# Retention by feature: keys in both layouts, queries as the moving operand, heads and gates as column tiles of the array

## The chip, the cores and the metric

The kernel runs on one core of a Trainium2 chip. The metric is the time of one execution on the device in microseconds. Effects of a few microseconds are compared through medians.

In the views PE is TensorE, PEld its weight loads, DVE VectorE, ACT ScalarE, POOL GpSimd. In a matmul the operand `lhsT` is loaded as weights and stays (stationary), while `rhs` streams past (moving). A record is one line of the trace; a float32 matmul of the source leaves two. With the shape of the array I mean rows*columns of the weights, as 128*64 in a view.

## The reference

A retention layer is followed by a mixture of experts with one expert per token. The change concerns the first part and the gate logits.

```python
# q, k, v: (B=8, H=8, S=576, 64)
gamma = 1.0 - 2.0 ** (-5.0 - np.arange(H))
rel = pos[:, None] - pos[None, :]
Dmat = np.where(rel >= 0, gamma[:, None, None] ** rel, 0.0)
ret = (q @ k.T / 8) * Dmat
x = (ret @ v)                      # then (B, S, 512)
logits = x @ w_gate                # 8 experts
local_gate = sigmoid(x @ w_local)  # 1 more column
# ... each token through relu(x @ w1[e]) @ w2[e], times its softmax share
```

## The kernel before

The 4608 tokens go in 36 chunks of 128; nine chunks are a pair of sequences. The decay gamma^(t-s) is split into a factor on the queries' side and one on the values. So a chunk needs masked scores times values inside the chunk, queries times a running state for what came before, and an update of that state. Everything is float32. The parts that the change touches:

```python
def scores(i):
    ld = raw.tile([P, 3, D], F32)              # q by feature; k, v by token
    nc.sync.dma_start(out=ld, in_=qkv[i])
    for c in range(4):                         # keys by feature, on TensorE
        nc.tensor.transpose(kps[:, c, :], kn[:, c * P:(c + 1) * P], ident)
    nc.scalar.copy(kT, kps)
    # vs = v * key decay (GpSimd)
    for c in range(4):
        for u in range(2):                     # two heads in two row halves
            nc.tensor.matmul(sps[u][:, c, :], lhsT=kT[r, c, :], rhs=qT[r, c, :], ...)
    # sT = sps * mask (VectorE)

def outputs(i):
    for h in range(8):                         # scores stationary, values moving
        nc.tensor.matmul(ops[:, h, :], lhsT=sT[:, h % 2, h // 2, :],
                         rhs=vs[:, h * DH:(h + 1) * DH], ...)
    for c in range(4):                         # queries stationary, state moving
        nc.tensor.matmul(ops[...], lhsT=qT[:, c, 0:n], rhs=state[:, c, :], ...)
    for c in range(4):                         # two heads against two: half is thrown away
        nc.tensor.matmul(kv[:, c, :], lhsT=kn[r, c * P:(c + 1) * P],
                         rhs=vs[r, c * P:(c + 1) * P], ...)
    # state = diagonal blocks of kv (ScalarE); x = ops * query decay; x to DRAM

def logits(i):
    for c in range(4):
        nc.tensor.transpose(xps[:, c, :], x[:, c * P:(c + 1) * P], ident)
    nc.scalar.copy(xT, xps)
    for c in range(4):
        nc.tensor.matmul(lps[:, i, :], lhsT=xT[:, c, :], rhs=wg[:, c, :], ...)
# cut: the routing (which expert each token takes), then 25 blocks of 256 slots through experts
```

## Time and profile before

| | before |
|---|---|
| median of 4 runs, us | 1038.82 (1037.56 to 1039.0) |
| retention, to the last gate matmul | 250.3 us |
| routing and experts | the rest, 787 us |

Two groups of retention in the costliest-groups view, and the load of a chunk in the list of DMA issues. In a group, the shapes after the names are weights and moving operand (partitions x elements). Then come the count of records, busy time in us, mean ns of one, idle time before them and what ended it.

```profile
L139 PE MATMUL ops<-vs,sT 128*128 128x64 f32 x576 | 82.3, 277 | 0.0
L112 PE MATMUL kps<-ident,ld 128*128 128x128 f32 x144 | 22.6, 281 | 6.2 <-DMA ld<-in_qkv_dram 6.2
...
ld<-in_qkv_dram SPq DMA_DIRECT2D x36, 768.0 KB, 4.5
```

The first is the target: 576 records of intra-chunk outputs, each loading 128 columns of weights to stream only 64. The second is the key transposes. Neither waits for anything after the first loads. The third tells that a chunk's load lands in 4.5 us, while a chunk takes 6.6.

### The profile page before, as it was taken

How to read it: one execution, taken by the hardware profiler on the slowest of the kernel's cores; microseconds unless marked ns; L12 is line 12 of the kernel's file. 1: busy time of each engine (PE TensorE's matmuls, PEld its weight loads, DVE VectorE, ACT ScalarE, POOL GpSimd, SP SyncE). 2: the span in 40 equal slices, each digit the busy share in tenths (PEclk: the TensorE clock that was granted, in tenths of full speed). 3: DMA queues.
4: the chain of work that ended last, by engine and by line, in shares of the span. 5: the costliest groups of instructions: out<-in, count | busy, mean ns of one | idle time of the engine just before them, and what ended most of it. 6: DMA issues, size and time to landing. Idle time of an engine off the chain costs nothing. (4 is left out here: it accounts for less than half of the span.)

```text
span 1037.5 us, 12062 instructions
## 1 busy us (share of the span) xinstructions
PE 974.9 (94%) x4918; PEld 719.0 (69%) x4918; DVE 166.8 (16%) x282; ACT 123.8 (12%) x238; POOL 140.7 (14%) x158
## 2 busy tenths in 40 slices
PE   7999999996479999999999999999999999999995
PEld 6999999995466666666666666666666666666662
DVE  2333332324711111010111111010111110010100
ACT  2222222221000000000000000000000000000000
POOL 2111111110021111011111110011111110110000
PEclk9999999998589999999999999999999999999998
DMA  5444444430735544555455544555455544555300
GB/s 201 154 158 157 151 163 162 163 133 32 273 122 203 201 156 148 185 197 177 153 179 187 193 156 153 181 193 188 138 187 203 164 158 160 195 183 167 127 2 0
DMA packets 47509, 166.03 MB, mean 160 GB/s; under 512 B 7006, under 2 KB 7134, under 8 KB 47456
## 3 DMA queue, kind: packets, MB, share of 16 engines
q1 hardware_dynamic: 39168, 142.62, 40.5%
q0 software_dynamic: 8000, 22.56, 6.3%
q8 instruction: 39, 0.64, 0.2%
q14 instruction: 14, 0.11, 0.0%
q10 hardware_dynamic: 288, 0.09, 0.0%
HBM read 146.37 MB, written 22.54 MB: 163 GB/s over the span
## 5 line engine op out<-in xcount | busy, mean ns | idle before, releaser
L395 PE MATMUL hps<-xTs,w1s 128*128 128x256 f32 x1600 | 353.2, 382 | 14.1 <-DVE xTs L389 14.1
L402 PE MATMUL yps<-w2s,hT 128*128 128x512 f32 x800 | 347.4, 592 | 0.0
L395 PEld LDWEIGHTS hps<-xTs,w1s 128*128 128x128 f32 x1600 | 303.0, 191 | 60.2 <-DVE xTs L389 19.8
L402 PEld LDWEIGHTS yps<-w2s,hT 128*128 128x128 f32 x800 | 152.0, 190 | 180.7 <-issue 179.4
L405 DVE TENSOR_SCALAR y<-yps,pslot 128x512 f32<-128x512 f32 x50 | 37.5, 751 | 665.4 <-PE yps L402 665.4
L397 ACT ACTIVATE hT<-hps 128x512 f32<-128x512 f32 x100 | 59.7, 597 | 700.2 <-PE hps L395 700.2
L406 POOL DMA_INDIRECT out_dram<-y,sidx x50 | 50.7, 1014 | 512.0 <-DVE y L405 505.3
L139 PE MATMUL ops<-vs,sT 128*128 128x64 f32 x576 | 82.3, 277 | 0.0
L139 PEld LDWEIGHTS ops<-vs,sT 128*128 128x128 f32 x576 | 72.4, 191 | 4.9 <-issue 0.6
L127 DVE TENSOR_TENSOR sT<-sps,mask 128x512 f32<-128x512 f32 x72 | 46.4, 686 | 159.9 <-PE sps L123 159.9
L383 POOL DMA_INDIRECT xg<-xd,gidx x50 | 48.7, 975 | 164.0 <-PE xgps L388 121.2
L116 POOL TENSOR_TENSOR vs<-ld,dec 128x512 f32<-128x512 f32 x36 | 37.5, 1042 | 190.0 <-PE kv L155 173.2
L123 PE MATMUL sps<-ld,kT 64*128 64x128 f32 x576 | 43.2, 288 | 0.2 <-DVE sT L127 0.2
L161 ACT COPY state<-kv 64x256 f32<-64x256 f32 x64 | 23.4, 366 | 160.2 <-PE kv L155 159.4
L176 PE MATMUL lps<-wg,xT 128*128 128x9 f32 x288 | 38.0, 259 | 1.5 <-ACT xT L174 1.1
L176 PEld LDWEIGHTS lps<-wg,xT 128*128 128x128 f32 x288 | 34.9, 191 | 5.2 <-ACT xT L174 4.7
L123 PEld LDWEIGHTS sps<-ld,kT 64*128 64x128 f32 x576 | 36.3, 190 | 2.9 <-DVE sT L127 0.4
L388 PEld LDWEIGHTS xgps<-ident,xg 128*128 128x128 f32 x200 | 24.2, 146 | 20.1 <-issue 19.5
L155 PE MATMUL kv<-vs,ld 128*128 128x128 f32 (+1 forms) x256 | 35.5, 281 | 0.5 <-ACT state L161 0.5
L146 PE MATMUL ops<-state,ld 128*128 128x128 f32 (+1 forms) x256 | 35.4, 281 | 0.0
L388 PE MATMUL xgps<-ident,xg 128*128 128x128 f32 x200 | 27.7, 282 | 6.6 <-DMA xg<-xd,gidx 6.6
L389 DVE COPY xTs<-xgps 128x512 f32<-128x512 f32 x50 | 32.2, 682 | 7.1 <-PE xgps L388 7.1
(112 smaller groups left out, 271.2 us busy)
## 6 DMA issues: line engine op xcount, KB each, us to landing
w1s<-in_w_dram SPq DMA_DIRECT2D x100, 512.0 KB, 5.5
w2s<-in_w_dram SPq DMA_DIRECT2D x100, 512.0 KB, 8.1
ld<-in_qkv_dram SPq DMA_DIRECT2D x36, 768.0 KB, 4.5
xd<-x SPq DMA_DIRECT2D x36, 256.0 KB, 2.2
xg<-xd,gidx POOLq DMA_INDIRECT x50, 7.3
out_dram<-y,sidx POOLq DMA_INDIRECT x50, 7.5
dec<-in_decay_dram ACTq DMA_DIRECT2D x1, 72.0 KB, 4.6
wg<-in_wgl_dram ACTq DMA_DIRECT2D x1, 18.0 KB, 6.2
```

Of the source, the lines that this page charges most:

```text
L116: nc.gpsimd.tensor_tensor(vs.rearrange("p (h d) -> p h d", h=H), vn.rearrange("p (h d) -> p h d", h=H), dec[:, 1, m, :].unsqueeze(2).to_br ...
L123: nc.tensor.matmul(sps[u][:, c, :], lhsT=kT[r, c, :], rhs=qT[r, c, :], start=True, stop=True, skip_group_check=True)
L127: nc.vector.tensor_tensor(sT[:, u], sps[u], (mask2 if m == MID else mask).unsqueeze(1).to_broadcast([P, HP, P]), op=Alu.mult)
L139: nc.tensor.matmul(ops[:, h, :], lhsT=sT[:, h % 2, h // 2, :], rhs=vs[:, h * DH:(h + 1) * DH], start=(h == 0), stop=(m == 0), skip_group_c ...
L176: nc.tensor.matmul(lps[:, i, :], lhsT=xT[:, c, :], rhs=wg[:, c, :], start=(c == 0), stop=(c == DK - 1), skip_group_check=True)
L383: nc.gpsimd.indirect_dma_start(out=xg, out_offset=None, in_=xd, in_offset=bass.IndirectOffsetOnAxis(ap=gidx[:, s:s + 1], axis=0))
L388: nc.tensor.transpose(xps[:, c, :], xg[:, c * P:(c + 1) * P], ident)
L395: nc.tensor.matmul(hps[:, v, :], lhsT=w1s[:, m + v, c, :], rhs=xT[:, c, :], start=(c == 0), stop=(c == DK - 1), skip_group_check=True)
L397: nc.scalar.activation(hT[:, m:m + 2, :], hps, Act.Relu)
L402: nc.tensor.matmul(yps, lhsT=hT[:, m, u * P:(u + 1) * P], rhs=w2s[:, m, :], start=(m == 0), stop=(m == FK - 1))
L405: nc.vector.tensor_scalar(y, yps, pslot[:, s:s + 1], None, Alu.mult)
L406: nc.gpsimd.indirect_dma_start(out=out, out_offset=bass.IndirectOffsetOnAxis(ap=sidx[:, s:s + 1], axis=0), in_=y, in_offset=None, bounds_c ...
```

## The change: its intent and the diff

The products are turned round so that what is small becomes the weights. Values (64 columns) are stationary and scores move. Two heads then fit side by side in the left and right 64 columns of the array. The output comes by feature, as the gates need it, and is transposed to tokens for the store instead. Keys are loaded in both layouts, so no key is transposed on the chip. The gates' four partial products are four 32-column tiles, summed by one more matmul a chunk later.

```diff
-            ld = raw.tile([P, 3, D], F32, name="ld")
+            ld = raw.tile([P, 4, D], F32, name="ld")
-            for c in range(HP):
-                nc.tensor.transpose(kps[:, c, :], kn[:, c * P:(c + 1) * P], ident)
-            nc.scalar.copy(kT, kps)
+            kT = ld[:, 1].rearrange("p (c s) -> p c s", c=HP)
 ...
-            for h in range(H):
-                nc.tensor.matmul(ops[:, h, :], lhsT=sT[:, h % 2, h // 2, :],
-                                 rhs=vs[:, h * DH:(h + 1) * DH], ...)
+            for c in range(HP):
+                for u in range(2):
+                    r = slice(u * DH, (u + 1) * DH)
+                    h = 2 * c + u
+                    nc.tensor.matmul(ops[r, c, :], lhsT=vs[:, h * DH:(h + 1) * DH], rhs=sT[:, u, c, :], ...)
 ...
-                        lhsT=qT[:, c, 0:n], rhs=states[(i + 1) % 2][:, c, :],
+                    nc.tensor.matmul(ops[:, c, 0:n], lhsT=states[(i + 1) % 2][:, c, :], rhs=qT[:, c, 0:n], ...)
 ...
-                    nc.tensor.matmul(kv[:, c, :], lhsT=kn[r, c * P:(c + 1) * P],
-                                     rhs=vs[r, c * P:(c + 1) * P], ...)
+                    for u in range(2):      # r: rows of the output, h: one head, k: tokens
+                        nc.tensor.matmul(kv[r, c, :], lhsT=kn[k, h], rhs=vs[k, h], ...)
 ...
+        def rows(i):
+            for c in range(DK):
+                nc.tensor.transpose(xps[:, c, :], xT[:, c, :], ident)
+            nc.scalar.copy(x, xps.rearrange("p c d -> p (c d)"))
+            nc.sync.dma_start(out=xd[i * P:(i + 1) * P, :], in_=x)
+            for c in range(DK):
+                nc.tensor.matmul(gps[c * GW:(c + 1) * GW, :], lhsT=wg[:, c, :], rhs=xT[:, c, :], ...)
+            nc.scalar.copy(gs, gps)
         def logits(i):
+            nc.tensor.matmul(lps[:, i, :], lhsT=chunks[i]["gs"], rhs=four[:, 0:E + 1], ...)
```

The query decay, now along the free axis, is a table of nine pieces of 256 KB that is loaded at the start.

More of the change, by code (lines that the diff above doesn't have):

```diff
@@ L38 @@
 NOWHERE = 2 * NTOK
+GW = 32
 @with_exitstack
@@ L45 @@
     qkv: bass.AP,
-    decay: bass.AP,
+    dk: bass.AP,
+    dq: bass.AP,
     wgl: bass.AP,
@@ L75 @@
         work = pool(part, "work", 3)
-        ps_t = pool(part, "ps_t", 2, PSUM)
         ps_s = pool(part, "ps_s", 3, PSUM)
         ps_o = pool(part, "ps_o", 1, PSUM)
+        ps_x = pool(part, "ps_x", 1, PSUM)
+        ps_g = pool(part, "ps_g", 1, PSUM)
         ps_kv = pool(part, "ps_kv", 1, PSUM)
         ps_l = pool(part, "ps_l", 1, PSUM)
-        dec = once.tile([P, 2, PER, H], F32, name="dec")
-        nc.scalar.dma_start(out=dec.rearrange("p t m h -> p (t m h)"), in_=decay)
-        wg = once.tile([P, DK, E + 1], F32, name="wg")
+        deck = once.tile([P, PER, H], F32, name="deck")
+        nc.scalar.dma_start(out=deck.rearrange("p m h -> p (m h)"), in_=dk)
+        decq = once.tile([P, PER, HP, P], F32, name="decq")
+        for m in range(PER):
+            nc.scalar.dma_start(out=decq[:, m].rearrange("p c t -> p (c t)"), in_=dq[:, m])
+        wg = once.tile([P, DK, GW], F32, name="wg")
         nc.scalar.dma_start(out=wg.rearrange("p k e -> p (k e)"), in_=wgl)
+        four = once.tile([P, GW], F32, name="four")
+        nc.gpsimd.memset(four, 0.0)
+        for k in range(DK):
+            nc.vector.tensor_copy(four[k * GW:(k + 1) * GW], ident[k * GW:(k + 1) * GW, k * GW:(k + 1) * GW])
         mask = once.tile([P, P], F32, name="mask")
@@ L105, in scores @@
             g = chunks[i]
-            ld = raw.tile([P, 3, D], F32, name="ld")
+            ld = raw.tile([P, 4, D], F32, name="ld")
             nc.sync.dma_start(out=ld.rearrange("p t x -> p (t x)"), in_=qkv[i])
             qT = ld[:, 0].rearrange("p (c s) -> p c s", c=HP)
-            kn, vn = ld[:, 1], ld[:, 2]
-            kps = ps_t.tile([P, HP, P], F32, name="kps", tag="t")
-            for c in range(HP):
-                nc.tensor.transpose(kps[:, c, :], kn[:, c * P:(c + 1) * P], ident)
-            kT = work.tile([P, HP, P], F32, name="kT")
-            nc.scalar.copy(kT, kps)
+            kT = ld[:, 1].rearrange("p (c s) -> p c s", c=HP)
+            kn, vn = ld[:, 2], ld[:, 3]
             vs = work.tile([P, D], F32, name="vs")
@@ L117, in scores @@
                 vs.rearrange("p (h d) -> p h d", h=H), vn.rearrange("p (h d) -> p h d", h=H),
-                dec[:, 1, m, :].unsqueeze(2).to_broadcast([P, H, DH]), op=Alu.mult)
+                deck[:, m, :].unsqueeze(2).to_broadcast([P, H, DH]), op=Alu.mult)
             sps = [ps_s.tile([P, HP, P], F32, name=f"sps{u}", tag="s") for u in range(2)]
@@ L136, in outputs @@
             qT, kn, vs, sT = g["qT"], g["kn"], g["vs"], g["sT"]
-            ops = ps_o.tile([P, H, DH], F32, name="ops")
-            for h in range(H):
-                nc.tensor.matmul(ops[:, h, :], lhsT=sT[:, h % 2, h // 2, :],
-                                 rhs=vs[:, h * DH:(h + 1) * DH],
-                                 start=(h == 0), stop=(m == 0), skip_group_check=True)
+            ops = ps_o.tile([P, HP, P], F32, name="ops")
+            for c in range(HP):
+                for u in range(2):
+                    r = slice(u * DH, (u + 1) * DH)
+                    h = 2 * c + u
+                    nc.tensor.matmul(ops[r, c, :], lhsT=vs[:, h * DH:(h + 1) * DH], rhs=sT[:, u, c, :],
+                                     start=(c == 0), stop=(m == 0), skip_group_check=True)
             if m > 0:
@@ L145, in outputs @@
                 for c in range(HP):
-                    nc.tensor.matmul(
-                        ops[0:n, 2 * c:2 * c + 2, :].rearrange("p h d -> p (h d)"),
-                        lhsT=qT[:, c, 0:n], rhs=states[(i + 1) % 2][:, c, :],
-                        start=False, stop=True, skip_group_check=True)
+                    nc.tensor.matmul(ops[:, c, 0:n], lhsT=states[(i + 1) % 2][:, c, :], rhs=qT[:, c, 0:n],
+                                     start=False, stop=True, skip_group_check=True)
@@ L150, in outputs @@
             if m != PER - 1:
-                r = slice(HALF, P) if m == MID else slice(0, P)
+                k = slice(HALF, P) if m == MID else slice(0, P)
                 if m in (0, MID):
-                    kv = ps_kv.tile([P, HP, P], F32, name="kv")
+                    kv = ps_kv.tile([P, HP, DH], F32, name="kv")
                 for c in range(HP):
-                    nc.tensor.matmul(kv[:, c, :], lhsT=kn[r, c * P:(c + 1) * P],
-                                     rhs=vs[r, c * P:(c + 1) * P],
-                                     start=(m in (0, MID) and c == 0), stop=True,
-                                     skip_group_check=True)
+                    for u in range(2):
+                        r = slice(u * DH, (u + 1) * DH)
+                        h = slice((2 * c + u) * DH, (2 * c + u + 1) * DH)
+                        nc.tensor.matmul(kv[r, c, :], lhsT=kn[k, h], rhs=vs[k, h],
+                                         start=(m in (0, MID) and c == 0), stop=True,
+                                         skip_group_check=True)
@@ L159, in outputs @@
                 for u in range(2):
                     r = slice(u * DH, (u + 1) * DH)
-                    nc.scalar.copy(states[i % 2][r, :, r], kv[r, :, r])
-            g["x"] = x = work.tile([P, D], F32, name="x")
-            nc.vector.tensor_tensor(
-                x.rearrange("p (h d) -> p h d", h=H), ops,
-                dec[:, 0, m, :].unsqueeze(2).to_broadcast([P, H, DH]), op=Alu.mult)
-            nc.sync.dma_start(out=xd[i * P:(i + 1) * P, :], in_=x)
-        def logits(i):
-            x = chunks[i]["x"]
-            xps = ps_t.tile([P, DK, P], F32, name="xps", tag="t")
-            for c in range(DK):
-                nc.tensor.transpose(xps[:, c, :], x[:, c * P:(c + 1) * P], ident)
-            xT = work.tile([P, DK, P], F32, name="xT")
-            nc.scalar.copy(xT, xps)
-            for c in range(DK):
-                nc.tensor.matmul(lps[:, i, :], lhsT=xT[:, c, :], rhs=wg[:, c, :],
-                                 start=(c == 0), stop=(c == DK - 1), skip_group_check=True)
+                    nc.scalar.copy(states[i % 2][r, :, r], kv[r, :, :])
@@ new lines, in outputs @@
+            g["xT"] = xT = work.tile([P, HP, P], F32, name="xT")
+            nc.vector.tensor_tensor(xT, ops, decq[:, m], op=Alu.mult)
+        def rows(i):
+            xT = chunks[i]["xT"]
+            xps = ps_x.tile([P, DK, P], F32, name="xps")
+            for c in range(DK):
+                nc.tensor.transpose(xps[:, c, :], xT[:, c, :], ident)
+            x = work.tile([P, D], F32, name="x")
+            nc.scalar.copy(x, xps.rearrange("p c d -> p (c d)"))
+            nc.sync.dma_start(out=xd[i * P:(i + 1) * P, :], in_=x)
+            gps = ps_g.tile([P, P], F32, name="gps")
+            for c in range(DK):
+                nc.tensor.matmul(gps[c * GW:(c + 1) * GW, :], lhsT=wg[:, c, :], rhs=xT[:, c, :],
+                                 start=True, stop=True, skip_group_check=True)
+            gs = work.tile([P, P], F32, name="gs")
+            nc.scalar.copy(gs, gps)
+            chunks[i]["gs"] = gs
@@ L179 @@
+        def logits(i):
+            nc.tensor.matmul(lps[:, i, :], lhsT=chunks[i]["gs"], rhs=four[:, 0:E + 1],
+                             start=True, stop=True, skip_group_check=True)
         scores(0)
-        for i in range(NCH + 1):
+        for i in range(NCH + 2):
             if i + 1 < NCH:
@@ L184 @@
                 outputs(i)
-            if i > 0:
-                logits(i - 1)
+            if 0 <= i - 1 < NCH:
+                rows(i - 1)
+            if 0 <= i - 2 < NCH:
+                logits(i - 2)
         nc.vector.tensor_copy(lt, lps)
@@ L422, in _decay @@
 def _decay(np):
-    at = (np.arange(PER)[None, :] * P + np.arange(P)[:, None]) % S
+    at = np.arange(PER * P) % S
     gamma = 1.0 - 2.0 ** (-5.0 - np.arange(H))
-    power = gamma[None, None, :] ** at[:, :, None].astype(np.float64)
-    both = np.stack([power / math.sqrt(DH), 1.0 / power], 1)
-    return both.reshape(P, 2 * PER * H).astype(np.float32)
+    power = gamma[:, None] ** at[None, :].astype(np.float64)
+    dq = (power / math.sqrt(DH)).reshape(HP, 2, 1, PER, P) * np.ones((1, 1, DH, 1, 1))
+    dq = dq.transpose(1, 2, 3, 0, 4).reshape(P, PER, HP * P)
+    dk = (1.0 / power).reshape(H, PER, P).transpose(2, 1, 0).reshape(P, PER * H)
+    return dk.astype(np.float32), dq.astype(np.float32)
 def kernel(**inputs):
@@ L438 @@
     i = {n: _np.asarray(a) for n, a in inputs.items()}
-    gates = _np.concatenate([i["moe_w_gate"], i["moe_w_local"]], 1)
+    gates = _np.concatenate(
+        [i["moe_w_gate"], i["moe_w_local"], _np.zeros((D, GW - E - 1), _np.float32)], 1)
+    dk, dq = _decay(_np)
     arrays = {
         "qkv": _np.concatenate(
-            [_by_feature(i["q"], _np), _by_token(i["k"], _np), _by_token(i["v"], _np)], 2),
-        "decay": _decay(_np),
-        "wgl": gates.reshape(DK, P, E + 1).transpose(1, 0, 2).reshape(P, DK * (E + 1)),
+            [_by_feature(i["q"], _np), _by_feature(i["k"], _np),
+             _by_token(i["k"], _np), _by_token(i["v"], _np)], 2),
+        "dk": dk,
+        "dq": dq,
+        "wgl": gates.reshape(DK, P, GW).transpose(1, 0, 2).reshape(P, DK * GW),
         "w1": i["moe_w1"].reshape(E, DK, P, FK, P).transpose(0, 2, 3, 1, 4).reshape(E, P, FK * D),
```

## The prediction

> **What bounds the kernel now.** I read the page first, its line of busy tenths: it shows three stages. These are the first ten slices (a slice is 1037.5 / 40 = 26 us), a dip, and the experts. The change touches the first stage, retention, alone.
>
> ```profile
> PE   7999999996479999999999999999999999999995
> ...
> PEclk9999999998589999999999999999999999999998
> ```
>
> TensorE is at 9 (90% or more) in both long stages, at full clock. The dip is the routing, on VectorE. The busy time of every engine in a stretch of 26 us in mid-retention says what limits that stage:
>
> ```profile
> 130.00:156.00 26.00, 25.96 (x250) 24.83 (x249) 7.83 (x12) 6.60 (x16) 4.12 (x4) 1.00 0.50 166
> ```
>
> The columns are PE, PEld, DVE, ACT, POOL, then granted clock, DMA share, GB/s. PE is busy for 25.96 of 26 us; the vector engines are below a third, DMA at half. So what a part of the change saves or costs on PE moves the end, and nothing else does, as long as no engine or queue comes near PE. Next, the timeline of PE over one whole chunk of 128 tokens:
>
> ```profile
> 112.28 1.16 PE L123 MATMUL sps<-ld,kT 64*128 64x128 f32 x16
> 113.37 0.66 PE L139 MATMUL ops<-vs,sT 128*128 128x64 f32 x4
> 113.86 1.11 PE L146 MATMUL ops<-state,ld 128*128 128x128 f32 x8
> 114.81 1.06 PE L155 MATMUL kv<-vs,ld 128*128 128x128 f32 x8
> 115.70 0.60 PE L172 MATMUL xps<-ident,x 128*128 128x128 f32 x4
> 116.14 0.60 PE L112 MATMUL kps<-ident,ld 128*128 128x128 f32 x4
> 116.58 0.78 PE L139 MATMUL ops<-vs,sT 128*128 128x64 f32 x6
> 117.38 1.06 PE L176 MATMUL lps<-wg,xT 128*128 128x9 f32 x8
> 118.29 0.86 PE L139 MATMUL ops<-vs,sT 128*128 128x64 f32 x6
> 119.08 1.16 PE L123 MATMUL sps<-ld,kT 64*128 64x128 f32 x16
> ```
>
> The first column is the start; since durations overlap, I take differences of starts. There is no wait in it: one chunk is 119.08 - 112.28 = 6.80 us of 64 records. A matmul of the source is two records in float32 (8 score matmuls, x16), a transpose is one. The records cost what their weights cost, not what they stream: lps with 9 moving columns takes 0.91 / 8 = 0.114 us, kv with 128 takes 0.89 / 8 = 0.111. Over nine chunks (first and last of a pair of sequences do less) stores of x go out at 108.92 and 168.60: 59.68 / 9 = 6.63 us a chunk. The last gate matmul ends at 250.3.
>
> Two exceptions carry my argument. **The scores run in pairs already.** They have K = 64 and alternate between the two halves of the rows: x16 takes 1.09 us, 0.068 each. In the trace their single starts are 7 ns apart within a pair, 112 ns from pair to pair. **One 64-column tile alone gains nothing, and a switch costs.** At the chunk of two sequences the state product has 64 weight columns, all in one half of the array:
>
> ```profile
> 100.08 1.09 PE L146 MATMUL ops<-state,ld 128*64 128x128 f32 x8
> 101.10 1.16 PE L155 MATMUL kv<-vs,ld 64*128 64x128 f32 x8
> 102.18 0.66 PE L172 MATMUL xps<-ident,x 128*128 128x128 f32 x4
> ```
>
> These take 1.02 and 1.08 us, where the full shapes take 0.95 and 0.89. From single starts there, 64-column records come 109 ns apart, set by the 128 moving columns; at each change of array shape one step is some 200 ns rather than 112, and the next 160 to 207. So a change of shape costs 0.14 to 0.19 us, 0.15 as my mean.
>
> **What the Trainium skill says.** (1) "TensorE: Matmul & The Clock Gate", section LDWEIGHTS: a load takes columns / 1.2 ns whatever K is, so 107 ns for 128 and 53 for 64. The trace agrees on the first (0.111 a record, weight-bound). (2) The same page, Part 3, measured speedup: three 32-column tiles with N = 512 gained 2.38x, about as row tiles do. This trace has the row tiles; it has no two column tiles together, so concurrency in float32 is an extrapolation. (3) "TensorEngine Tiling (Array Packing)", Key Properties: changing the tiling mode drains TensorE. The trace agrees, with the 0.14 to 0.19 us above. (4) "DMA: Bandwidth & Descriptors", Queues, rings and completion order: an engine takes turns between queue rows a packet at a time. This matters for the start only; no run before shows two loaded queues there.
>
> **The change part by part**, in PE time of a chunk, at 0.112 us a full record or a pair of tiles.
> - Scores: unchanged, 8 pairs, 0.90.
> - Key transposes removed, as keys come by feature too: before 0.44, after 0. An ACT copy of 0.59 goes with them.
> - Intra-chunk outputs: weights are now values with 64 columns, moving is the score tile of 128, two heads in two column halves. Before 16 records x 0.112 = 1.79; after 8 pairs x 0.112 = 0.90 if the halves overlap.
> - State product: roles swapped, still full, 8 x 0.112 = 0.90; 0.80 on average over nine chunks, as one has none.
> - kv: before 8 full records, 0.89, half of whose product was thrown away. After, 16 records of 64 x 64 in pairs. Weights and stream are both 53 ns, so 8 x 0.056 = 0.45 at best; if issue binds (the scores issue a load or matmul each 28 ns) 32 x 0.028 = 0.90. I take 0.65, so 0.58 on average.
> - Transposes of x stay, 0.44, now from feature to token, and ACT copies x out of PSUM for the store.
> - Gates: before 8 full records, 0.89. After, 8 records in four 32-column tiles: 2 x 0.112 = 0.22 at best, 0.45 if issue binds (I take 0.33), an ACT copy of 128x128, and one matmul to sum the four, 2 x 0.112 = 0.22.
> - Shape changes: before two of weight per chunk, into and out of the scores, part of the 6.63. After, the compiled order of PE is scores, ops, state, kv, xps, gps, lps, never interleaved: 7 changes in a chunk, 5 where state or kv is missing, so 6.6 x 0.15 = 0.98.
>
> Sum: 0.90 + 0.90 + 0.80 + 0.58 + 0.44 + 0.33 + 0.22 + 0.98 = 5.15 us, against 6.63. That is 1.48 us less; over the 34 chunks between the second store and the last, 50 us.
>
> Beside PE, per chunk: DVE keeps three passes of 0.69, 2.07; ACT has 2 x 0.37 + 0.59 + about 0.3 = 1.65; POOL 1.04. All are far below 5.15. Walking through the order with one PSUM buffer each for ops, xps, gps and kv, every reader is done more than 1.5 us before PE wants the buffer again. Gates are summed one chunk later than made, so lps finds its copy ready. I expect no wait of PE on an engine.
>
> DMA: a chunk loads 1.05 MB rather than 0.79 and stores 0.26: 1.31 MB / 5.15 us = 254 GB/s. Before, 166 GB/s were a share of 0.50; linearly 0.77.
>
> Start: at the start of before, loads of 768 KB were first used at 5.34, 7.26 and 9.15 us, so one each 1.9 us (414 GB/s). After, loads of 1 MB take 2.5 us alone, or 5 while 2.36 MB of query decay (nine DMAs) share the engines. The first scores then start at about 7.5 us, the second at 12, the third at 16; but no transpose and copy precede them. The second chunk's x would be ready at about 20 us; before, its store went out at 22.1. So about 2 us more gain, and the tail (about 3 us) is as before. In all 52 us, less 1 for what I overlook: 1039 - 51 = **988 us**. Routing and experts are untouched.
>
> **The rivals.**
> (a) Column tiles don't overlap in float32: matmuls in the two halves follow each other at 0.109. Then ops cost 1.75, gates 0.87, kv 0.90: 5.15 + 0.85 + 0.54 + 0.28 = 6.82 a chunk, 0.2 above before, so about 1043 us: within 2%. For it: the lone 64-column tile above gained nothing. Against: row halves overlap fully here. Chance 0.1.
> (b) Shape changes cost more with column tiles, say 0.30 each, with a weight load of every tile exposed: 1 us more a chunk, 1024 us, within 2%. For it: steps of 207 ns follow the drain of row tiles. Chance 0.07 in full; in part it is the upper end of my range.
> (c) DMA becomes the bound: 1.31 MB at the 330 GB/s that a share of 1.0 would give (166 / 0.50) is 4.0 us, below 5.15. Then nothing is lost; but if PE were as quick as 4.8 it would still not bind. I give it the start, 3 to 5 us. Slower than before would need 36 chunks at 200 GB/s: chance 0.02.
> (d) No issue limit, cheap switches (0.10): 5.15 - 0.2 - 0.1 - 0.33 = 4.5 us a chunk, 965 us. Chance 0.08.
>
> **Range and chances.** The known parts of the sum (scores, ops, state, transposes, lps) are 3.26 us; the doubtful ones (kv, gates, switches) are 1.89, uncertain by about +0.5 and -0.4, so +17 and -14 us. The range is 974 to 1008. Faster by over 2% means below 1018: all of my case, and part of (b). Chances 0.88, 0.09, 0.03.
>
> **What would show it.** Right: retention's last gate matmul ends near 199 us rather than 250; PE still above 95% busy in mid-retention; ops x16 in about 0.9 us plus a switch, starts in pairs; kv x16 between 0.5 and 0.9; DMA share 0.7 to 0.8. Wrong: ops x16 near 1.8 us (rival a); gaps above 0.25 us at each change of shape (b); scores waiting on a load in mid-retention (c); PE waiting on ACT for xps or gps, which I excluded. The expert stage should last as long as before; if it doesn't, my reading that the stages are separate is wrong.

## More of the kernel before

The kernel before was less steady: in one call 6 of its 11 runs took 1045 us and 5 took 1038 to 1040, in another 2 of 7 took 1045, all at granted clocks of 0.977 to 0.981.

## The result and the profile after

The changed kernel took 979.04 us (median of 4 runs, 977.95 to 982.49) against 1038.82. The ratio is 0.9432, 95% interval 0.9414 to 0.9449. A ratio here is the mean time of one kernel's fast runs over that of the other's in the same rounds, so it is not quite the ratio of the two medians. The time lies 9 us below the predicted 988, inside its range.

The busy tenths of TensorE, and every engine's busy time in the same stretch as before (PE, PEld, DVE, ACT, POOL, clock, DMA share, GB/s):

```profile
PE   6999999727999999999999999999999999999995
```

```profile
130.00:156.00 26.00, 26.00 (x370) 21.68 (x370) 10.46 (x16) 8.20 (x22) 5.21 (x5) 1.00 0.80 269
```

The first stage is now nearly eight slices of 24 us (190.8 us), and TensorE is still busy throughout it but for the start. It has 370 records in 26 us instead of 250. DMA is at 0.80, and between 30 and 180 us the trace shows no wait of TensorE's matmuls for a load. One chunk with all its parts, on the timeline of PE (start, duration):

```profile
106.38 1.16 PE L131 MATMUL sps<-ld 64*128 64x128 f32 x16
107.47 1.09 PE L151 MATMUL ops<-sT,vs 128*64 128x128 f32 x16
108.49 1.16 PE L157 MATMUL ops<-ld,state 128*128 128x128 f32 x8
109.58 0.69 PE L167 MATMUL kv<-vs,ld 128*64 128x64 f32 x16
110.20 0.65 PE L180 MATMUL xps<-ident,xT 128*128 128x128 f32 x4
110.78 0.42 PE L186 MATMUL gps<-xT,wg 128*32 128x128 f32 x8
111.14 0.39 PE L193 MATMUL lps<-four,gs 128*128 128x9 f32 x2
111.46 1.16 PE L131 MATMUL sps<-ld 64*128 64x128 f32 x16
```

The chunk takes 111.46 - 106.38 = 5.08 us instead of 6.80. The 16 intra-chunk records take 1.02 us with one change of shape; before they took 2.08 in three pieces. The 16 key-value records take 0.62 us. In the trace's single starts, the intra-chunk records come in pairs 7 ns apart, 109 ns from pair to pair; the key-value ones in pairs every 58 ns; the gates four at a time within 20 ns, the second four starting 133 ns after the first.

The start looks different. From the full timeline:

```profile
5.88 2.08 PE L131 MATMUL sps<-ld 64*128 64x128 f32 x16 [5.88 <-DMA ld<-in_qkv_dram]
...
9.05 2.67 PE L131 MATMUL sps<-ld 64*128 64x128 f32 x16 [1.09 <-DMA ld<-in_qkv_dram]
...
16.85 2.08 PE L131 MATMUL sps<-ld 64*128 64x128 f32 x16 [2.38 <-DMA ld<-in_qkv_dram]
...
20.76 1.88 PE L157 MATMUL ops<-ld,state 128*128 128x128 f32 x8
...
22.68 0.69 DVE L174 TENSOR_TENSOR xT<-ops,decq 128x512 f32<-128x512 f32 x1 [2.46 <-PE ops L157]
```

The bracket is the idle time before the group and what ended it. TensorE waits for the second and third chunk. The group of 16 that takes 1.16 us in mid-stage takes 2.08 here, and the state product 1.88 instead of 1.16: the array runs at half pace. The trace's clock records begin, at full clock, 22.3 us into the span; in the kernel before they begin at 11.1. This one profile is not the whole story, as the part on the start shows.

### The profile page after: what moved, and what is told of

The parts are those of the page before. It is cut to its first block, busy times and chain, and to the rows that moved or that the text cites. A ratio compares the mean times of both kernels' runs of the same rounds, so it can differ in the third digit from the quotient of the medians.

```text
span 977.2 us, 12437 instructions
## 1 busy us (share of the span) xinstructions
PE 913.9 (94%) x5102; PEld 641.8 (66%) x5102; DVE 167.0 (17%) x286; ACT 112.1 (11%) x238; POOL 140.3 (14%) x159
## 5 line engine op out<-in xcount | busy, mean ns | idle before, releaser
L414 PE MATMUL hps<-xTs,w1s 128*128 128x256 f32 x1600 | 353.0, 381 | 14.1 <-DVE xTs L408 14.1
L124 POOL TENSOR_TENSOR vs<-ld,deck 128x512 f32<-128x512 f32 x36 | 37.5, 1042 | 136.2 <-DMA ld<-in_qkv_dram 92.4
L131 PE MATMUL sps<-ld 64*128 64x128 f32 x576 | 45.2, 297 | 9.3 <-DMA ld<-in_qkv_dram 9.3
L131 PEld LDWEIGHTS sps<-ld 64*128 64x128 f32 x576 | 38.0, 199 | 10.7 <-DMA ld<-in_qkv_dram 7.3
L151 PE MATMUL ops<-sT,vs 128*64 128x128 f32 x576 | 41.1, 287 | 0.0
L157 PE MATMUL ops<-ld,state 128*128 128x128 f32 (+1 forms) x256 | 37.6, 291 | 0.0
L157 PEld LDWEIGHTS ops<-ld,state 128*128 128x128 f32 x256 | 31.7, 195 | 5.6 <-issue 5.6
L151 PEld LDWEIGHTS ops<-sT,vs 128*64 128x64 f32 x576 | 32.1, 141 | 4.5 <-issue 0.4
L174 DVE TENSOR_TENSOR xT<-ops,decq 128x512 f32<-128x512 f32 x36 | 24.9, 691 | 31.4 <-PE ops L157 30.4
L367 PE MATMUL slots<-col,row 128*128 128x100 f32 x72 | 11.1, 331 | 13.6 <-DVE col L358 13.6
```

The lines of the kernel that those rows point to most:

```text
L124: nc.gpsimd.tensor_tensor(vs.rearrange("p (h d) -> p h d", h=H), vn.rearrange("p (h d) -> p h d", h=H), deck[:, m, :].unsqueeze(2).to_broa ...
L151: nc.tensor.matmul(ops[r, c, :], lhsT=vs[:, h * DH:(h + 1) * DH], rhs=sT[:, u, c, :], start=(c == 0), stop=(m == 0), skip_group_check=True)
L157: nc.tensor.matmul(ops[:, c, 0:n], lhsT=states[(i + 1) % 2][:, c, :], rhs=qT[:, c, 0:n], start=False, stop=True, skip_group_check=True)
L414: nc.tensor.matmul(hps[:, v, :], lhsT=w1s[:, m + v, c, :], rhs=xT[:, c, :], start=(c == 0), stop=(c == DK - 1), skip_group_check=True)
```

## The experiments

All kernels gave the right result. Differences are from the changed kernel, 979.04 us (978.44 in the rows after_again to late_decay).

| label | what | median us | difference |
|---|---|---|---|
| ops_serial | loop of the output heads turned | 994.04 | +15.0 |
| kv_serial | loop of the key-value heads turned | 986.77 | +7.7 |
| gates_full | gates as before | 981.87 | +2.8 |
| keys_back | keys transposed on chip | 996.75 | +17.7 |
| after_again | unaltered | 978.44 | 0 |
| kv_first | 5 changes of shape for 7 | 971.53 | -6.9 |
| four_switches | 4 changes for 7 | 964.34 | -14.1 |
| late_decay | decay table loaded piece by piece | 972.35 | -6.1 |
| ops_split | output halves kept apart | 1009.23 | +30.2 |
| kv_full | key-value products as before | 984.28 | +5.2 |
| best1 | four_switches and late_decay | 959.87 | -19.2 |
| best2 | best1, first loads in two pieces | 964.75 | -14.3 |

My theory: the gain comes from column halves running at once, from the key transposes left out, and less from the rest; changes of the array's shape take part of it back. The main rivals are that narrow weights alone are the gain, and that the gaps between groups are waits that would be there anyway.

### Do the halves run at once? ops_serial, kv_serial, ops_split

The first try turned the loop, so that neighbours share a half:

```diff
-            for c in range(HP):
-                for u in range(2):
+            for u in range(2):
+                for c in range(HP):
```

> The changed kernel with one loop turned round: the intra-chunk products of the even heads (left 64 columns) all come before those of the odd heads (right 64 columns). Same instructions, same shapes. Theory (the gain comes from two halves of the array running at once, which needs neighbours in different halves): the 16 records of a chunk follow each other at 0.109 us instead of going in pairs, 1.74 us instead of 0.87, so +0.87 us a chunk, 36 chunks: +31 us, about 1010 us. Rival (the gain is from the narrower weights alone, or the array overlaps whatever the order): 979 us, unchanged.

It took 994.04 us, half of the expected loss, between theory and rival. The timeline of PE shows why:

```profile
109.39 1.25 PE L151 MATMUL ops<-sT,vs 128*64 128x128 f32 x13
110.38 0.27 PE L167 MATMUL kv<-vs,ld 128*64 128x64 f32 x1
110.48 0.27 PE L151 MATMUL ops<-sT,vs 128*64 128x128 f32 x1
110.49 0.22 PE L167 MATMUL kv<-vs,ld 128*64 128x64 f32 x1
110.59 0.27 PE L151 MATMUL ops<-sT,vs 128*64 128x128 f32 x1
```

In the program, all 16 output records precede the key-value records. In the trace, key-value records of the left half start between the last output records of the right half. One half overtakes the other, measured against the order of the program. Whether the array does this or the compiled order of instructions is not shown: the compiled order is not on record, and it moves matmuls elsewhere (late_decay below). Among the outputs too, single starts show five left records alone, 109 ns apart, then right ones joining 6 ns behind. So turning the loop did not take the overlap away, only part of it, and this run alone could not decide.

> The same turn of the loop for the key-value state alone (64 weight columns, 64 moving). Theory: the records follow each other at 0.058 us, 16 in 0.93 us instead of 0.46, in 32 of 36 chunks: +15 us, about 994. If a half cannot load its next weights while it streams, up to 0.11 a record and +28 us or so more. Rival (already limited by the issue of instructions): unchanged, 979.

The same turn for the key-value products cost 7.7 us, again half of what I expected, and their single starts overtake in the same way. A chunk with all parts took 115.27 - 109.91 = 5.36 us on its timeline instead of 5.08.

So a third kernel put full-array work between the halves:

```diff
-            for c in range(HP):
-                for u in range(2):      # both halves of the outputs
             # state product first, start=(c == 0)
+            intra(0)                    # left half
+            rows(i - 1)                 # the transposes of the chunk before
+            intra(1)                    # right half
```

> The changed kernel with the two halves of the intra-chunk outputs really apart: the four heads of the left half, then the transposes of the chunk before (full array), then the four heads of the right half; the state product goes ahead of both. Same instructions, same result, 7 changes of shape in a chunk with all parts as before (one or two more at the ends of a pair of sequences, 0.05 us a chunk on average). Full-array work between keeps one half from overtaking the other, as it did when only the loop was turned. Theory: 16 records one after another at 0.109, +0.87 us a chunk, up to 0.2 given back by the key-value products overtaking: 24 to 33 us more, 1002 to 1012 us. Rival (narrow weights are the gain): 979 to 981.

```profile
112.50 1.09 PE L152 MATMUL ops<-sT,vs 128*64 128x128 f32 x8
113.52 0.66 PE L185 MATMUL xps<-ident,xT 128*128 128x128 f32 x4
114.10 1.09 PE L152 MATMUL ops<-sT,vs 128*64 128x128 f32 x8
115.12 0.42 PE L194 MATMUL gps<-xT,wg 128*32 128x128 f32 x8
```

Now 8 records take as long (1.02 us each group) as the 16 did. A full chunk elsewhere in this trace took 110.32 - 104.38 = 5.94 us, 0.86 more than 5.08, for the 0.87 of the theory. The loss is 30.2 us; theory said 24 to 33, the rival 0 to 2. The narrow weights by themselves gain nothing for the outputs: the overlap of the two halves is worth 30 us of the 60.

### What the other parts are worth: keys_back, kv_full, gates_full

keys_back loads three layouts again and transposes keys two chunks ahead, beside the state product:

```diff
+            kn, vn = ld[:, 1], ld[:, 2]
+            for c in range(HP):
+                nc.tensor.transpose(kps[:, c, :], kn[:, c * P:(c + 1) * P], ident)
+            nc.scalar.copy(kT, kps)
```

> The changed kernel with keys loaded by token alone and transposed on TensorE again, two chunks ahead, next to the state product so that no change of array shape is added (only in the 4 to 8 chunks without a state product). Theory (PE-bound; keys by feature save just the four transposes): +0.44 us a chunk, +16 us, less 1 to 3 us for a start with a quarter less to load: 992 to 995. Rival 1 (the larger loads cost what the transposes saved): 979 or less. Rival 2 (the copy of the transposed keys on ScalarE was a wait of its own): over 1000.

It took 996.75 us, 2 above my range. A full chunk took 108.90 - 103.43 = 5.47 us on its timeline, 0.39 more than 5.08. From the second chunk's x to the last chunk's a chunk took 5.245 us on average for 4.856, over 34 chunks 13.2 us. The other 4.8 us of the trace's loss lie before the second x, where I expected a gain:

```profile
12.68 1.28 ACT L125 ACT_TABLE_LOAD   x1 [12.68 <-DMA decq<-in_dq_dram]
13.97 1.07 ACT L125 COPY kT<-kps 128x512 f32<-128x512 f32 x2
...
14.61 5.01 PE L140 MATMUL sps<-ld,kT 64*128 64x128 f32 x32 [3.51 <-ACT kT L125]
```

ScalarE issues the nine loads of the decay table before it copies the first keys. So the first scores started at 14.61 us instead of 5.88, after a wait of 3.51 us for that copy: rival 2 was true at the start, and only there. Part of the 4.8 us is this wait and part the first transposes themselves; the run doesn't tell their shares apart. DMA fell from 0.81 to 0.59 of its time between 52 and 156 us without any use. So the larger load is free there. The transposes are worth 13 us from the second x on, and less than 18 in all.

kv_full goes back to eight full key-value records, half thrown away:

```diff
-                    for u in range(2):
-                        nc.tensor.matmul(kv[r, c, :], lhsT=kn[k, h], rhs=vs[k, h], ...)
+                    nc.tensor.matmul(kv[:, c, :], lhsT=kn[k, c * P:(c + 1) * P], rhs=vs[k, c * P:(c + 1) * P], ...)
```

> The changed kernel with the key-value products as before, 8 full records of which half is thrown away, instead of 16 in two 64-column halves. Theory: 0.89 instead of 0.46 us, but in the 28 chunks that have a state product two changes of shape fall away, 0.30: 28 x 0.13 + 4 x 0.43 = 5 us more, about 984. Rival (changes of shape cost nothing): 32 x 0.43 = 14 us more, 993.

984.28 us, as the theory has it and not the rival. On its timeline a full chunk takes 112.48 - 107.27 = 5.21 us. Half the records cost almost as much as the tiles here, because the tiles need a change of shape on each side.

> The changed kernel with the gates computed as before (the token-feature tile stationary, nine gate columns moving, 8 full records), so no 32-column tiles, no copy of their result, no summing matmul. Theory: 0.89 us of full records takes the place of 0.22 + 0.22 and of two changes of array shape, 0.30: +0.15 us a chunk, +5 us, 984. Rival (changes of shape cost nothing, the four tiles are all gain): +0.45 us a chunk, +16 us, 995.

The gates as before (edit: the eight full records of the old logits read xT, and the tiles, their copy and the summing matmul go) took 981.87 us, +2.8 for the expected +5. On its timeline a chunk takes 114.02 - 108.82 = 5.20 us, 0.12 more for the expected 0.15, which would be 4.3 us over 36 chunks. Most of the remaining 1.5 is in the tail: without the extra step for the sum, the last gate matmul ended 1.39 us after the last x instead of 2.36. The four tiles, which look like a large saving, are worth almost nothing where they stand.

### Do the changes of shape cost time by themselves? kv_first, four_switches

kv_first moves the key-value products up, next to the outputs of the same shape; not one instruction is added or removed:

```diff
-            if m > 0:                   # state product
-                ...
             if m != PER - 1:            # key-value products
                 ...
+            if m > 0:
+                ...
```

four_switches also puts the summing gate matmul before the gate tiles, next to the transposes:

```diff
             rows(i - 1)                 # transposes only
             logits(i - 2)               # the summing matmul
+            gates(i - 1)                # the four tiles
```

> The changed kernel once more, unaltered, so that the small differences of this call are taken on one chip: 977 to 982 us.

The unaltered kernel took 978.44 us (976.08 to 980.68).

> The changed kernel with the key-value products moved from behind the state product to before it, next to the intra-chunk products of the same array shape. Nothing else changes; a chunk that has both then changes the array's shape 5 times instead of 7 (28 of 36 chunks). Theory (each change costs about 0.15 us by itself): 28 x 2 x 0.15 = 8 us less, about 971. Rival (the gaps at the borders of groups are waits for semaphores or the first weights, and come with every group whatever its shape): unchanged, 979.

> As kv_first, and the summing gate matmul of the chunk two back, a full shape, goes before the four-column-tile gates instead of behind them, next to the transposes of the same shape: 4 changes of shape instead of 7. Theory: 36 x 0.15 = 5 us more than kv_first, about 965 us. Rival: unchanged, 979.

They took 971.53 and 964.34 us: 6.9 and 14.1 less. Below is a chunk of four_switches on the timeline of PE, from outputs to the next scores.

```profile
108.47 1.09 PE L151 MATMUL ops<-sT,vs 128*64 128x128 f32 x16
109.39 0.64 PE L161 MATMUL kv<-vs,ld 128*64 128x64 f32 x16
109.95 1.16 PE L168 MATMUL ops<-ld,state 128*128 128x128 f32 x8
110.95 0.60 PE L181 MATMUL xps<-ident,xT 128*128 128x128 f32 x4
111.39 0.29 PE L197 MATMUL lps<-four,gs 128*128 128x9 f32 x2
111.60 0.43 PE L190 MATMUL gps<-xT,wg 128*32 128x128 f32 x8
111.96 1.16 PE L131 MATMUL sps<-ld 64*128 64x128 f32 x16
```

Outputs now take 109.39 - 108.47 = 0.92 us where 1.02 were, transposes 0.44 where 0.58 were: the gap is gone wherever the next group has the same shape, and stays where it has not. The groups and their dependencies are the same, so the rival falls. The chunk is 111.96 - 107.37 = 4.59 us against 5.08: three changes fewer save 0.49, so 0.16 each. In kv_first it is 112.55 - 107.77 = 4.78, 0.30 less for two changes.

### The start: late_decay, and the best versions

```diff
-        for m in range(PER):
-            nc.scalar.dma_start(out=decq[:, m]..., in_=dq[:, m])
             nc.sync.dma_start(out=ld..., in_=qkv[i])
+            if i < PER:
+                nc.sync.dma_start(out=decq[:, i]..., in_=dq[:, i])
```

> The changed kernel with each 256 KB piece of the query decay loaded behind the chunk that needs it, on the same queue, instead of nine at the very start on another queue. Theory (they share the engines with the first three chunks, TensorE waits 1.1 and 2.4 us more for these and then runs some microseconds at half pace): the second and third chunk land at about 8 and 12 us instead of 9 and 17, 4 to 6 us less, about 974. Rival (the first chunks land no sooner, as 1 MB each is what takes the time): 978 to 979.

It took 972.35 us, 6.1 less than after_again, where 4 to 6 were expected.

```profile
8.07 1.11 PE L167 MATMUL kv<-vs,ld 128*64 128x64 f32 x14
9.42 1.98 PE L131 MATMUL sps<-ld 64*128 64x128 f32 x16 [0.24 <-DMA ld<-in_qkv_dram]
...
13.80 1.16 PE L131 MATMUL sps<-ld 64*128 64x128 f32 x16
```

The third chunk's scores start at 13.80 us rather than 16.85 and run at full pace; the clock records begin at 11.2 us. Two things came together here. The table no longer competes with the chunks' loads, and the compiled order moved 14 key-value records ahead of the second scores, which filled the gap. This run does not tell their shares apart. Against the expectation the second chunk landed no sooner (its scores start at 9.42 us, before at 9.05); only the third did.

How long the half pace lasts is not fixed by the kernel alone. after_again, the same kernel, was at full clock from 13.9 to 17.3 us, then at half until 20.7, and its second x was ready at 22.35 us rather than 23.37. The runs with the early decay table (keys_back apart, whose start differs) can be sorted by the idle time of TensorE before the third scores. Where it was 2.3 to 3.1 us (the two of the changed kernel, gates_full, kv_serial, kv_first, four_switches), half pace lasted or came back until 20.7 to 23.3 us. Where it was 1.5 to 1.6 us (ops_serial, ops_split, kv_full), the clock was full from 14.9 to 15.9 us on; kv_full, for one:

```profile
16.82 1.16 PE L131 MATMUL sps<-ld 64*128 64x128 f32 x16 [1.53 <-DMA ld<-in_qkv_dram]
```

So a longer gap and half pace go together in nine profiles. No run changed the gap alone.

> four_switches and late_decay together. Theory (one shortens every chunk, the other the start): 14 + 6 = 20 us less than the changed kernel, 958 to 960. Rival (the shorter chunk makes the loads the bound): 964 as with four_switches alone.

best1 took 959.87 us, as the sum said. It beats the changed kernel by 19 us and the kernel before by 78 (against the lower of two clusters of before; the ratio, 0.9211, is flattered by the upper one). In the stretch from 26 to 156 us its DMA share is 0.92 at 305 GB/s, and beside the first load the waits of its scores for loads sum to 1.4 us. Of these 1.1 lie after 26 us, where the changed kernel has none: a sign, not a proof, that the loads are the next bound.

> best1 with the first two chunks' loads in two pieces each, queries and keys by feature first, so that the first scores start about 1 us sooner: 957 to 959. If the first scores still wait for the whole, as best1.

best2 (first two loads split in two) failed: 964.75 us. The first scores did start sooner, at 5.24 us for 5.93. But the compiled order then spread the second chunk's work so that the clock records begin at full clock only at 17.8 us, not 10.6, and outputs of 16 records took 1.97 us meanwhile. Its second x was ready at 22.49 us for 17.93, which is nearly the whole loss. Why the half pace lasted so long is not shown; a wait of 1.36 us for the second load stood in it, where best1 waited 0.25.

## Why the prediction was right, point by point

**What bounds.** Right. Retention is bound by TensorE before and after, and nothing else took its place. Routing and experts last 786 us (977.2 less 190.8) against 787 (1037.5 less 250.3).

**Overlap of halves in float32**, the extrapolation of the prediction and its rival (a). Right: predicted 0.90 us for the outputs' eight pairs, measured 8 x 0.109 = 0.87. ops_split shows it as a cause and not only as a pattern. (In the sum of rival (a) the 0.28 for kv should be 0.22 to 0.25 by its own terms, 0.90 against 0.65 in eight or nine of nine chunks. It changes nothing.)

**Key transposes.** Right in the chunk: 0.44 us predicted, 0.39 in keys_back's full chunk. Its 17.7 us hold more than that, a start that the copy on ScalarE made worse.

**Changes of shape.** Right. With the spacings above, and 0.22 taken for the two steps of the gates and of the sum each, a full chunk without changes is 0.90 + 0.87 + 0.90 + 0.46 + 0.44 + 0.22 + 0.22 = 4.01 us. Seven changes are the rest of 5.08, 0.153 each on average; I had put 0.15. kv_first and four_switches confirm it by taking them away. Rival (b) fell.

**kv and gates: the mis-sized terms.** I feared that records could not be issued closer than the scores' 28 ns per load or matmul, and took 0.65 us for kv and 0.33 for the gates. They took 0.46 and about 0.21 (0.36 on the timeline, less a change of 0.15): their best cases, and so half of rival (d), to which I had given 0.08. This is -0.19 and -0.11 of the -0.31 by which a full chunk was shorter than my terms (5.08 against 0.90 + 0.90 + 0.90 + 0.65 + 0.44 + 0.33 + 0.22 + 7 x 0.15 = 5.39). Over the 34 chunks from the second x to the last (23.37 to 188.45 us in the trace) a chunk took 4.86 us for my average of 5.15: 10 us.

**The start.** Wrong in sign. I expected the second chunk's x ready at 20 us, 2 us ahead of before; it came at 23.37, 1.3 behind. Of the load times the third was guessed well (scores at 16 predicted, 16.85 measured); the first two came sooner than I said (5.88 and 9.05 for 7.5 and 12). What I left out is the half pace, in this profile until 22.3 us: some 3 us lost. In kv_full, with the same loads but full pace from 14.9 us, the second x was ready at 20.83, near my 20. The tail was about 1 us shorter than before. Together: -10 + 3.4 - 1 = -8 us on the last gate matmul, predicted at 199 and seen at 190.8. With the 1 us I had kept in reserve, that is the miss of 9. So the number is good partly because the start's loss hid a third of what the chunks gained beyond the forecast.

**Waits on other engines and DMA.** Right: none in mid-stage. DMA at 0.80 (predicted 0.77); ScalarE's new copy takes 0.272 us (I put 0.3).

Of the 60 us, then, the overlap of the outputs is worth 30, the keys 13 to 18, the key-value tiles 5 and the gate tiles 3. This is 51 to 56, and since each was undone alone they need not add up.

## What to carry to other kernels

Where float32 matmuls have weights of 64 columns, as the outputs here, put two in the two column halves and issue them alternately: a pair then took 0.109 us, and so did one alone. Count the changes of array shape in the loop (0.15 us each here) and order the groups by shape; here that was worth 14 us for no other edit, and without it narrow tiles around few records (the gates) gained almost nothing. A table needed only piece by piece should not be loaded ahead of the first work: loading it late was worth 6 us here. Look at which engine issues it, too; in keys_back ScalarE's first key copy stood behind it until 12.7 us.

## What the Trainium skill lacked or had wrong

- "TensorE: Matmul & The Clock Gate", Part 3, "What overlaps and what doesn't", says that matmuls keep strict program order in start and end. Whether this holds between tiles in different column halves stays open here: in ops_serial, key-value records of the left half start at 110.38 and 110.49 us, ahead of output records at 110.48 and 110.59 that precede both in the kernel's text, but the compiled order is not on record.
- "TensorEngine Tiling (Array Packing)", Key Properties, names the drain at a change of tiling mode but no cost. Here a change costs 0.153 us (7 in a chunk of 5.08), and three fewer save 0.49.
- No page that I used gives the pace of float32 column tiles in a loop where every matmul loads new weights. In these runs a pair of 128-column streams in two halves takes 109 ns, and the key-value records, which stream 64 columns, come at 29 ns each on average.
- The profile rather than a page: the granted clock is printed as 1.00 for the first 22 us of the changed kernel, where its trace has no clock record yet and matmuls take twice as long (2.08 for 1.16 us).
